# Seven block products for the second channel layer too, on one core

## The chip, the cores and the metric

One core of one Trainium2 chip runs the kernel in a single launch. The metric is the device time of one execution in microseconds (us). The engines are named as the profile names them: PE (TensorE, matrix products into PSUM), DVE (VectorE), ACT (ScalarE), POOL (GpSimd), SP (SyncE, which only issues transfers here). Each takes its instructions in the order in which they stand in its own queue, and semaphores join the queues.

## The reference

The input is `x`, 8 sequences of 3008 tokens with 256 features. A Fourier mixing comes first (`rfft` over the tokens, a complex 256 x 256 product, a soft threshold, `irfft`), then a layer over the tokens, then one over the channels:

```python
xt = x.transpose(0, 2, 1)
h = np.maximum(xt @ w_tok1, 0.0) @ w_tok2
u = x + h.transpose(0, 2, 1)
h2 = np.maximum(u @ w_ch1, 0.0) @ w_ch2      # 256 -> 1536 -> 256
return (u + h2).astype(np.float32)
```

The change is in the last two lines: for each token the channel layer takes `u` (256 features) to 1536 hidden values, rectifies them, takes them back to 256 and adds `u`.

## The kernel before

All products are of float32 quality, from two parts: a tensor is held as `hi` (rounded to the shorter format that the fast matmul takes) and `lo` (the rest), and a product is three matmuls, hi x hi, hi x lo and lo x hi (`mm3`, lines 195 to 198). "Product" below always means these three.

**Stages.** The first half, some 1200 us, computes the Fourier mixing and the token layer of the sequences (units 0 to 4: two of one sequence, three of two), and does the channel layer of the first units beside it, in chunks of at most 512 tokens (`channel`). The rest of the tokens are done in 17 **wide chunks** of up to 1024 (`CW7`) in `channel7`; this is the second half of the time. What the wide chunks need of earlier stages (`g`, `b_d`, `wt2_d`) is in DRAM or SBUF by then. In each wide chunk `make_u` forms `u` for the next one from groups of up to 470 tokens (12 matmuls of that width in each half of a group, and up to ten short ones), ACT copies it to `uf`, `sum_u` makes four sums of its blocks on DVE, and `split_u7` splits the seven operands into hi and lo (`ub`; ACT makes hi, DVE lo).

**First layer by seven products.** The 2 x 2 blocks of the first weight matrix (two feature halves by two hidden blocks of 128) and of `u` (two feature halves by two halves of the chunk's tokens, up to 512 each) are multiplied by seven products in place of eight, in a scheme of Strassen's kind: sums of weight blocks (`ws`, made by `weigh` in the last narrow chunk) times sums of blocks of `u`. `first7(n, p)` does this for one pair `p` of hidden blocks; there are six pairs. The products go to four banks of PSUM (`sx`, `sw`, `sq`, `sz`; `sx` is written three times). ACT and DVE bring the partial sums to SBUF (`sn`), and `rectify` makes hi and lo of the rectified hidden block (`hh` on ACT, `hlo` on DVE).

**Second layer by plain products.** `second7` multiplies each of the 12 hidden blocks, for each token half, with the two output halves of its weights (`w2h`, `w2l`, resident in SBUF) and sums over all 12 in PSUM (`po`, four banks). So a chunk has 42 products in the first layer and 48 in the second. `finish7` adds `uf` and stores the chunk.

**Order.** The code is a loop over pairs: `first7` of a pair, `second7` of the pair before, `make_u` of the next chunk in between. A scheduler puts each engine's instructions in order from that; PE's too, within the dependencies.

## Time and profile before

| | |
|---|---|
| three runs | 2392.57, 2396.88 and 2397.1 us; median 2396.88 |
| the profiled execution | span 2395.2 us from the first to the last instruction; its own time is known by this span alone, 1.7 us under the median of the runs |
| instructions | 32192, of them 12542 matmuls |
| granted PE clock | 0.998 in the mean |
| PE waits for another engine, wide stage | none listed between 1205 us and the end |
| DMA | 173 GB/s up to 1200.6 us, 57 GB/s from there to 2379.7 us |

How to read it: "busy" of an engine counts its instructions' time from start to end; a matmul's end is modelled, and one starts before the last has ended, so a sum of durations says less of PE than the distance between starts. Where PE never waits, the other engines' idle time costs nothing.

### The profile page before, as it was taken

What the parts mean: (1) busy time and instruction counts of PE and PEld (TensorE: products, weight loads), DVE (VectorE), ACT (ScalarE), POOL (GpSimd) and SP (SyncE); (2) the same over time, 40 slices, a digit from 0 to 9 for tenths busy, and PEclk for the clock granted to TensorE, in tenths of its full rate; (3) what the DMA queues carried; (4) which work ended last, traced back from release to release, by engine and by line L of the source; (5) the groups of instructions that cost most, each with busy time, mean ns of one, the idle gap of its engine ahead of it and who ended that gap; (6) DMA issues with size and microseconds to landing.
All of it is one profiled execution on the core that took longest, in us unless ns stands there. A gap on an engine that the chain in (4) does not pass through costs nothing.

```text
span 2395.2 us, 32192 instructions
## 1 busy us (share of the span) xinstructions
PE 2361.0 (99%) x12542; PEld 2065.4 (86%) x12542; DVE 1401.9 (59%) x2189; ACT 1129.6 (47%) x2002; POOL 252.5 (11%) x223
## 2 busy tenths in 40 slices
PE   8999999999999999999999999999999999999999
PEld 7878998999888888899888888898888889888887
DVE  7976666655546554655555555555555555555554
ACT  6764445544435443434344444444444444444543
POOL 0000332222213221222000000000000000000000
PEclk9999999999999999999999999999999999999999
DMA  8875477655555554442413112121211112221100
GB/s 210 253 230 155 164 226 220 187 177 165 162 166 159 157 170 159 135 156 97 131 53 90 57 55 62 31 82 60 91 57 38 56 53 82 60 87 61 39 1 35
DMA packets 149767, 277.06 MB, mean 116 GB/s; under 512 B 10934, under 2 KB 94734, under 8 KB 149614
## 3 DMA queue, kind: packets, MB, share of 16 engines
q1 hardware_dynamic: 115225, 208.40, 29.4%
q10 hardware_dynamic: 34388, 66.60, 8.2%
q8 instruction: 99, 1.62, 0.3%
q14 instruction: 55, 0.44, 0.1%
HBM read 177.57 MB, written 97.39 MB: 115 GB/s over the span
## 4 chain that ended last, share of the span: by engine, by line
PE 88%; DVE 4%; DMA 4%; ACT 2%; issue 1%; SPq 1%; POOL 0%; ACTq 0%; DVEq 0%; POOLq 0%
PE po L196 10%; PE po L197 10%; PE po L198 10%; PE pu L860 5%; PE sx L196 3%; PE sx L197 3%; PE sx L198 3%; PE px L482 3%; PE ph L196 3%; PE ph L198 3%; PE ph L197 2%; PE pm L196 2%; PE pm L198 2%; PE pm L197 2%; PE sw L196 2%; PE sw L197 2%
## 5 line engine op out<-in xcount | busy, mean ns | idle before, releaser
L196 PE MATMUL po<-hh,w2h 128*128 128x512 f32 (+5 forms) x1176 | 453.5, 386 | 1.2 <-DVE o L965 0.9
L197 PE MATMUL po<-hlo,w2h 128*128 128x512 f32 (+5 forms) x1176 | 449.9, 383 | 3.3 <-DVE hlo L899 3.3
L198 PE MATMUL po<-hh,w2l 128*128 128x512 f32 (+5 forms) x1176 | 449.6, 382 | 0.0
L1032 ACT ACTIVATE hh<-sn 128x512 fp32r<-128x512 f32 (+2 forms) x408 | 256.2, 628 | 81.7 <-DVE sn L1052 53.3
L1033 DVE SCALAR_TENSOR_TENSOR hlo<-sn,hh 128x512 fp32r<-128x512 f32 (+2 forms) x408 | 275.4, 675 | 9.4 <-ACT hh L1032 0.7
L197 PEld LDWEIGHTS po<-hlo,w2h 128*128 128x128 f32 x1176 | 221.6, 188 | 40.7 <-DVE hlo L899 4.5
L196 PEld LDWEIGHTS po<-hh,w2h 128*128 128x128 f32 x1176 | 221.4, 188 | 38.2 <-ACT xf L484 1.0
L198 PEld LDWEIGHTS po<-hh,w2l 128*128 128x128 f32 x1176 | 221.4, 188 | 37.9
L1041 DVE TENSOR_TENSOR sn<-sq,sn 128x512 f32<-128x512 f32 (+2 forms) x102 | 69.5, 682 | 272.5 <-PE sq L198 255.2
L1037 ACT COPY sn<-sx 128x512 f32<-128x512 f32 (+2 forms) x102 | 59.2, 580 | 323.8 <-PE sx L198 323.8
L899 DVE SCALAR_TENSOR_TENSOR hlo<-ph,hh 128x512 fp32r<-128x512 f32 (+4 forms) x180 | 114.2, 637 | 108.5 <-ACT hh L898 107.1
L149 DVE TENSOR_TENSOR xtl<-xf,xth 128x768 fp32r<-128x768 f32 x84 | 85.2, 1014 | 116.4 <-ACT xth L146 116.1
L898 ACT ACTIVATE hh<-ph 128x512 fp32r<-128x512 f32 (+4 forms) x180 | 100.0, 557 | 112.2 <-PE ph L198 107.3
L196 PE MATMUL pm<-wmh,xth 128*128 128x256 f32 x504 | 145.7, 289 | 3.8 <-ACT xth L146 2.1
L867 ACT COPY uf<-pu 128x470 f32<-128x470 f32 (+16 forms) x152 | 60.5, 425 | 181.2 <-PE pu L860 180.5
L197 PE MATMUL pm<-wml,xth 128*128 128x256 f32 x504 | 142.5, 283 | 0.0
L198 PE MATMUL pm<-wmh,xtl 128*128 128x256 f32 x504 | 142.4, 284 | 0.0
L196 PE MATMUL ph<-uh,w 128*128 128x512 f32 (+4 forms) x360 | 137.1, 382 | 3.9 <-DVE hlo L899 3.2
L860 PEld LDWEIGHTS pu<-g,b 96*128 96x128 f32 x1024 | 130.8, 192 | 3.6 <-DMA b<-b_d 0.3
L197 PE MATMUL ph<-ul,w 128*128 128x512 f32 (+4 forms) x360 | 133.8, 372 | 0.0
L198 PE MATMUL ph<-uh,w 128*128 128x512 f32 (+4 forms) x360 | 133.8, 372 | 0.0
L860 PE MATMUL pu<-g,b 96*128 96x94 f32 x1024 | 129.3, 272 | 0.0
(185 smaller groups left out, 5128.7 us busy)
## 6 DMA issues: line engine op xcount, KB each, us to landing
wt<-wt_d SPq DMA_DIRECT2D x28, 940.0 KB, 5.7
x<-in_x SPq DMA_DIRECT2D x39, 480.0 KB, 4.6
wt<-ws_d SPq DMA_DIRECT2D x36, 512.0 KB, 3.8
a<-a_d SPq DMA_DIRECT2D x36, 512.0 KB, 5.4
b_d<-bt ACTq DMA_DIRECT2D x36, 512.0 KB, 5.1
a_d<-a ACTq DMA_DIRECT2D x36, 480.0 KB, 3.8
wt<-wt_d SPq DMA_DIRECT2D x21, 752.0 KB, 5.0
b<-b_d SPq DMA_DIRECT2D x32, 480.0 KB, 6.4
```

The lines of the kernel that those rows point to most:

```text
L149: lo_eng.tensor_tensor(out=lo, in0=src, in1=hi.bitcast(F32), op=ALU.subtract)
L196: PE.matmul(out, lhsT=wh, rhs=xh, start=start, stop=False, skip_group_check=more)
L197: PE.matmul(out, lhsT=wh, rhs=xl, start=False, stop=False, skip_group_check=more)
L198: PE.matmul(out, lhsT=wl, rhs=xh, start=False, stop=stop, skip_group_check=more)
L482: PE.matmul(pt[:, o:o + 128], lhsT=x, rhs=f2cols(2 * kp + ab), start=True, stop=True)
L860: PE.matmul(pt[:, s * TOKS:(s + 1) * TOKS], lhsT=b2[:, s, cs], rhs=g2[:, 0 if s0 + s == 0 else 1], start=False, stop=s == k - 1)
L867: S.copy(out=ufs[m][:, ct, lo - at:hi - at], in_=pt[:, lo - c0:hi - c0])
L898: S.activation(out=hh, in_=pt, func=AF.Relu)
L899: V.scalar_tensor_tensor(out=hlo, in0=pt, scalar=0.0, in1=hh.bitcast(F32), op0=ALU.max, op1=ALU.subtract)
L1032: S.activation(out=hh, in_=t, func=AF.Relu)
L1033: V.scalar_tensor_tensor(out=hlo, in0=t, scalar=0.0, in1=hh.bitcast(F32), op0=ALU.max, op1=ALU.subtract)
L1041: V.tensor_tensor(out=snap[0], in0=q, in1=snap[0], op=ALU.add)
```

## The change

`second7` now does the second layer by seven products too, over pairs of hidden blocks, token halves and output halves: a chunk has 42 products in either layer. To that end:

- `first7` leaves the four blocks of a pair (`c11`, `c22`, `r12`, `r21`) in float32 in SBUF, not split. It works on groups of three pairs (`TRIO`), and gives way after each product. One of the old snapshots goes, since the order of products is new and `sx` is written four times; three banks in place of four.
- The second layer works group by group, one group behind the first layer. For each of seven operands `r` and each of three pairs `k`, `prepare` makes the operand's sum (DVE) and its hi (ACT) and lo (DVE or POOL), five steps (`LEAD`) ahead, into one of six slots `rh`, `rl`. `product` multiplies it with weights that `weights2` loads from DRAM, three pairs summed in PSUM in one of three banks (`sbanks`). When an operand's three products are done, DVE adds the bank to a quarter of `uf`. In the second group the quarter is then stored.
- A step is one product of the first layer and one of the second, and these, with those of `u`, are pinned: PE runs them as the code writes them (`keep_in_program_order`). `u` has a bank of its own, and its halves are set at numbered steps.
- The sums of both layers' weights are made by `weigh` in the six chunks of unit 1, in 12 small pieces, and go to DRAM (`wsum_d`, `a2_d`); `keep_blocks` copies there those blocks of the second weights that are used as they are. The first layer's sums are read back in the last narrow chunk.

```diff
+TRIO = 3
+LEAD = 5
+AT = (0, 3, 4, 1, 5, 6, 2)
...
+            pt = wc["pu"] if pin else bank("pu")
             for jt in range(2):
-                mm3(pt[:, :n], gh[:, jt, b, cs], gl[:, jt, b, cs], w[:, jt, :n], w[:, 2 + jt, :n], jt == 0, False)
+                if pin:
+                    pinned(pt[:, :n], gh[:, jt, b, cs], gl[:, jt, b, cs], w[:, jt, :n], w[:, 2 + jt, :n], jt == 0)
+                else:
+                    mm3(pt[:, :n], gh[:, jt, b, cs], gl[:, jt, b, cs], w[:, jt, :n], w[:, 2 + jt, :n], jt == 0, False)
+                m = PE.matmul(pt[:, s * TOKS:(s + 1) * TOKS], lhsT=b2[:, s, cs], rhs=g2[:, 0 if s0 + s == 0 else 1], start=False, stop=s == k - 1, skip_group_check=pin)
+                if pin:
+                    tc.keep_in_program_order(m)
...
+            if n in early_sums and f in (4, 8):
+                weigh(*early_sums[n][f // 8])
+            if n in early_sums and f == 11 and early_sums[n][0][0]:
+                keep_blocks(early_sums[n][0][1] // 4)
...
+                if seven and 4 <= f < 10:
+                    DMA.dma_start(out=wc["ws"][:, f - 4].rearrange("p k h f -> p (k h f)").bitcast(F32), in_=wsum_d[:, f - 4])
-                if seven and f in (1, 3, 5):
-                    weigh(f // 2)
...
+    def weigh(kind, p):
...
+        V.tensor_tensor(out=a, in0=both[0].bitcast(F32), in1=both[1].bitcast(F32), op=ALU.add)
+        a11, a12, a21, a22 = (a[:, j, i * 128:(i + 1) * 128] for i in range(2) for j in range(2))
+        s1, s2, s3, s4 = (sf[:, i] for i in range(4))
...
+        V.tensor_tensor(out=s3, in0=a11, in1=a21, op=ALU.subtract)
+        V.tensor_tensor(out=s4, in0=a12, in1=s2, op=ALU.subtract)
+        split(so[:, :, 0], so[:, :, 1], sf, S, V)
+        if kind == 0:
+            DMA.dma_start(out=wsum_d[:, p], in_=so.rearrange("p k h f -> p (k h f)").bitcast(F32))
...
+            DMA.dma_start(out=a2_d[g].rearrange("r p k w -> k p r w")[k, :, 3:], in_=so.rearrange("p k h f -> p k (h f)").bitcast(F32))
+    def keep_blocks(g):
+        for r, (i, j) in enumerate(((0, 0), (0, 1), (1, 1))):
+            for n, name in enumerate(("w2h", "w2l")):
+                fs = wc[name][:, 2 * TRIO * g:2 * TRIO * (g + 1)].rearrange("p (k j) c -> p k j c", j=2)
+                DMA.dma_start(out=a2_d[g, r][:, :, n * 128:(n + 1) * 128], in_=fs[:, :, j, i * 128:(i + 1) * 128].bitcast(F32))
...
+    def pinned(out, wh, wl, xh, xl, start):
+        for n, (w, x) in enumerate(((wh, xh), (wh, xl), (wl, xh))):
+            m = PE.matmul(out, lhsT=w, rhs=x, start=start and n == 0, stop=n == 2, skip_group_check=True)
+            tc.keep_in_program_order(m)
+    def first7(n, g):
-        x, w, q, z = (bank(k)[:, :h] for k in ("sx", "sw", "sq", "sz"))
...
-            pos[n] = [ps1.tile([128, 2, 512], F32, tag=tag, name="po") for tag in ("po", "gp")]
-        for k in order:
-            hh, hlo = hs[f, k]
-            for ct in range(2):
-                cs = slice(ct * 128, (ct + 1) * 128)
-                mm3(pos[n][k][:, ct, :h], wc["w2h"][:, 2 * p + f, cs], wc["w2l"][:, 2 * p + f, cs], hh, hlo, p + f == 0, 2 * p + f == NF - 1)
...
+        for k in range(TRIO):
+            p = TRIO * g + k
+            c11, c22, r12, r21 = (t[:, k, :h] for t in blocks)
+            x, w, q = (bank(name)[:, :h] for name in ("sx", "sw", "sq"))
...
+            def product(out, a, i, start):
+                pinned(out, *left(p, a), ubs[i][:, 0, :h], ubs[i][:, 1, :h], start)
+            product(x, 4, 0, True)
+            S.copy(out=c11, in_=x)
+            yield
+            product(w, 0, 1, True)
+            S.copy(out=c22, in_=w)
+            yield
+            product(x, 1, 2, False)
+            S.copy(out=r12, in_=x)
+            yield
+            product(q, 5, 3, True)
+            V.tensor_tensor(out=c11, in0=q, in1=c11, op=ALU.add)
+            yield
+            product(x, 2, 4, False)
+            V.tensor_tensor(out=c22, in0=x, in1=c22, op=ALU.add)
+            yield
+            product(w, 3, 5, False)
+            V.tensor_tensor(out=r12, in0=w, in1=r12, op=ALU.add)
+            S.activation(out=r12, in_=r12, func=AF.Relu)
+            yield
+            product(x, 6, 6, False)
+            S.activation(out=r21, in_=x, func=AF.Relu)
+            yield
+    def weights2(g, r):
+        a = wc["seven"].tile([128, TRIO, 2, 128], F32R, name="a2s", bufs=3)
+        DMA.dma_start(out=a.rearrange("p k h f -> p (k h f)").bitcast(F32), in_=a2_d[g, AT[r]].rearrange("p k w -> p (k w)"))
+        return a
...
+    def second7(n, g, blocks, odd):
+        banks = wc["sbanks"]
+        x, w, q = (banks[i][:, :h] for i in ((2, 1, 0) if odd else (0, 1, 2)))
+        outs = (x, w, x, q, x, w, x)
+        homes = ((0, 0), (1, 1), (0, 1), (0, 0), (1, 1), (0, 1), (1, 0))
+        weights, ready = {}, {}
...
+        def prepare(j, slot):
+            r, k = divmod(j, TRIO)
+            hi, lo = (wc[name][:, slot, :h] for name in ("rh", "rl"))
+            a, b, c, d = (t[:, k, :h] for t in blocks)
+            src = (a, a, a, d, c, b, a)[r]
+            if r == 1:
+                V.scalar_tensor_tensor(out=a, in0=a, scalar=0.0, in1=c, op0=ALU.max, op1=ALU.subtract)
+            if r == 2:
+                V.scalar_tensor_tensor(out=a, in0=b, scalar=0.0, in1=a, op0=ALU.max, op1=ALU.add)
+            if r == 4:
+                V.scalar_tensor_tensor(out=c, in0=b, scalar=0.0, in1=c, op0=ALU.max, op1=ALU.subtract)
+            if r == 6:
+                V.tensor_tensor(out=a, in0=d, in1=a, op=ALU.subtract)
+            if r in (0, 5):
+                S.activation(out=hi, in_=src, func=AF.Relu)
+                V.scalar_tensor_tensor(out=lo, in0=src, scalar=0.0, in1=hi.bitcast(F32), op0=ALU.max, op1=ALU.subtract)
+            else:
+                S.copy(out=hi, in_=src)
+                eng = V if k == 0 and 2 <= r <= 4 else G
+                eng.tensor_tensor(out=lo, in0=src, in1=hi.bitcast(F32), op=ALU.subtract)
+            ready[j] = hi, lo
+        def product(j):
+            r, k = divmod(j, TRIO)
+            if k == 0:
+                fetch(r + 2)
+            hi, lo = ready.pop(j)
+            pinned(outs[r], weights[r][:, k, 0], weights[r][:, k, 1], hi, lo, r in (0, 1, 3) and k == 0)
+            if k == TRIO - 1:
+                i, j = homes[r]
+                o = uf[:, i, j * h:(j + 1) * h]
+                V.tensor_tensor(out=o, in0=outs[r], in1=o, op=ALU.add)
+                if g == 1 and r >= 3:
+                    store7(n, i, j)
+        return SimpleNamespace(prepare=prepare, product=product, fetch=fetch)
...
+        ps3 = ctx.enter_context(tc.tile_pool(name="ps3", bufs=1, space=bass.MemoryType.PSUM, reuse_waits="tile"))
+        wc["sbanks"] = [ps3.tile([128, 512], F32, name=f"s{i}") for i in range(3)]
+        wc["pu"] = ps3.tile([128, 512], F32, name="pu")
+        seconds, count = [], [-7 * TRIO]
...
+        def step():
+            j = count[0]
+            count[0] += 1
+            if j >= 0:
+                seconds[j // 21].product(j % 21)
+                if j % 21 in (19, 20) and j // 21 + 1 < len(seconds):
+                    seconds[j // 21 + 1].fetch(j % 21 - 19)
+            j += LEAD
+            if 0 <= j < 21 * len(seconds):
+                seconds[j // 21].prepare(j % 21, j % 6)
...
+                m = make_parts(g)
+                first = 1 + 6 * i if n == ns[0] else 22 - 9 * (len(mine) - 1 - i)
+                makes[first], makes[first + (3 if n == ns[0] else 4)] = (m, i), (m, i)
+            for g in range(2):
+                f = first7(n, g)
+                blocks = next(f)
+                seconds.append(second7(n, g, blocks, len(seconds) % 2))
+                for t in range(7 * TRIO):
+                    at = 7 * TRIO * g + t
+                    next(f)
+                    step()
+                    if at in makes:
+                        m, i = makes[at]
+                        if next(m, None) is not None and i + 1 < len(mine):
+                            load_wt2(mine[i + 1])
+                            load_b2(mine[i + 1])
+                    if at == 33:
+                        load_ahead(n + 2)
+                    if after:
+                        if at == 30:
+                            sum_u(after)
+                        if at in (32, 34):
+                            split_u7(after, at // 2 - 16)
+                        if at >= 37:
+                            split_u7(after, at - 35)
+        for _ in range(7 * TRIO):
+            step()
```

**The order on PE**, in the middle of the wide stage. Before, the seven products of a pair stand together (here the last two, into `sz` and `sx`), and behind them the eight of the second layer (`po`; `hh`, `hlo` are the hidden block's two parts):

```order
L196 MATMUL sz<-ub,w_963 128x512
L197 MATMUL sz<-ub,w_963 128x512
L198 MATMUL sz<-ub,w_963 128x512
L196 MATMUL sx<-ub,ws 128x512
L197 MATMUL sx<-ub,ws 128x512
L198 MATMUL sx<-ub,ws 128x512
L196 MATMUL po<-hh_18455,w2h 128x512
L197 MATMUL po<-hlo_18456,w2h 128x512
L198 MATMUL po<-hh_18455,w2l 128x512
```

Now (s_11429 and s_11431 are banks of the second layer, `a2s` its weights, `pu` the forming of `u`):

```order
L1059 MATMUL sx<-ub,ws 128x512 x3
L1059 MATMUL s_11429<-rh,a2s 128x512
L1059 MATMUL s_11429<-rl,a2s 128x512
L1059 MATMUL s_11429<-rh,a2s 128x512
L1059 MATMUL sw<-ub,ws 128x512 x3
L1059 MATMUL s_11431<-rh,a2s 128x512
L1059 MATMUL s_11431<-rl,a2s 128x512
L1059 MATMUL s_11431<-rh,a2s 128x512
L1059 MATMUL sx<-ub,w_965 128x512 x3
```

The two layers now alternate product by product, and between the end of one product into `sx` and the start of the next stand three others (two of the second layer, one into `sw`).

**The order on DVE**, from one add out of `sq` on, once a pair. Before (`hlo` is the lo of a hidden block, `sn` a partial sum):

```order
L1041 TENSOR_TENSOR sn<-sq,sn 128x512
L1046 TENSOR_TENSOR sn<-sw,sn 128x512
L1033 SCALAR_TENSOR_TENSOR hlo_16944<-sn,hh_16943 128x512
L1051 TENSOR_TENSOR sn<-sx,sn 128x512
L1033 SCALAR_TENSOR_TENSOR hlo_16952<-sn,hh_16951 128x512
L1052 TENSOR_TENSOR sn<-sx,sn 128x512
L1033 SCALAR_TENSOR_TENSOR hlo_16965<-sn,hh_16964 128x512
L1033 SCALAR_TENSOR_TENSOR hlo_16969<-sn,hh_16968 128x512
```

Now, the first 13 of the 16 instructions up to the next such add (c_18451 to r_18454 are the blocks of the group before, c_18744 and on those of the group in work):

```order
L1085 TENSOR_TENSOR c_18744<-sq,c_18744 128x512
L1124 SCALAR_TENSOR_TENSOR c_18451<-c_18452,c_18451 128x512
L1088 TENSOR_TENSOR c_18745<-sx,c_18745 128x512
L1135 TENSOR_TENSOR rl<-r_18454,rh 128x512
L1126 SCALAR_TENSOR_TENSOR r_18453<-c_18452,r_18453 128x512 x3
L1091 TENSOR_TENSOR r_18746<-sw,r_18746 128x512
L1147 TENSOR_TENSOR uf<-s_11430,uf 128x512
L1128 TENSOR_TENSOR c_18451<-r_18454,c_18451 128x512 x2
L1135 TENSOR_TENSOR rl<-r_18453,rh 128x512
L1128 TENSOR_TENSOR c_18451<-r_18454,c_18451 128x512
```

Four adds a pair out of the first layer's banks have become three (L1085, L1088, L1091), and between them now stand the preparation of the second layer's operands, with both inputs in SBUF, and the adds of finished outputs (L1147).

On POOL nothing stood in this stage; now it has 24 instructions a full chunk, all of one kind:

```order
L1135 TENSOR_TENSOR rl<-c_20170,rh 128x512 x3
L1135 TENSOR_TENSOR rl<-c_20456,rh 128x512 x5
L1135 TENSOR_TENSOR rl<-r_20459,rh 128x512 x2
L1135 TENSOR_TENSOR rl<-r_20458,rh 128x512 x2
L1135 TENSOR_TENSOR rl<-c_20456,rh 128x512 x3
```

They make the lo part of those operands that are not left to DVE (`eng` in `prepare`).

More of the change, by code (lines that the diff above doesn't have):

```diff
@@ L138, in tile_kernel @@
     ps = ctx.enter_context(tc.tile_pool(name="ps", bufs=4, space=bass.MemoryType.PSUM))
-    ps1 = ctx.enter_context(tc.tile_pool(name="ps1", bufs=1, space=bass.MemoryType.PSUM))
+    sums = ExitStack()
+    ps1 = sums.enter_context(tc.tile_pool(name="ps1", bufs=1, space=bass.MemoryType.PSUM))
     def bank(name):
@@ L1057, in tile_kernel @@
-    pos = {}
-    def second7(n, p, hs, f, order):
-        h = chunks[n][2] // 2
-        if n not in pos:
-            pos[n] = [ps1.tile([128, 2, 512], F32, tag=tag, name="po") for tag in ("po", "gp")]
-        for k in order:
-            hh, hlo = hs[f, k]
-            for ct in range(2):
-                cs = slice(ct * 128, (ct + 1) * 128)
-                mm3(pos[n][k][:, ct, :h], wc["w2h"][:, 2 * p + f, cs], wc["w2l"][:, 2 * p + f, cs], hh, hlo, p + f == 0, 2 * p + f == NF - 1)
-    def finish7(n, k, step):
+        blocks = [wc["tail"].tile([128, TRIO, CW], F32, tag="blk", name=k, bufs=8) for k in ("c11", "c22", "r12", "r21")]
@@ L1072, in finish7 @@
         uf = us[n][0]
[L1073 to L1080 removed]
+        for b, bi in enumerate(UNITS[u]):
+            lo, hi = max(at + j * h, b * N), min(at + (j + 1) * h, (b + 1) * N)
+            if lo < hi:
+                DMA.dma_start(out=outv[bi][:, i:i + 1, lo - b * N:hi - b * N], in_=uf[:, i:i + 1, lo - at:hi - at])
     def load_ahead(n):
@@ L1087, in load_ahead, with tasks_of @@
             load_b2(needs[n][0])
+    def tasks_of(first):
+        tasks = [(kind, p) for kind in range(2) for p in range(NF // 2)]
+        return {first + i: tasks[2 * i:2 * i + 2] for i in range(len(tasks) // 2)}
+    early_sums = tasks_of(min(n for n, (u, _, _) in enumerate(chunks) if u == 1))
     def channel7(ns):
@@ L1091, in channel7 @@
         wc["tail"] = ctx.enter_context(tc.tile_pool(name="tail", bufs=1, reuse_waits="tile"))
-        behind = None
-        half = NF // 2
+        for name, old in (("rh", "w2h"), ("rl", "w2l")):
+            wc[name] = const.tile([128, 2 * TRIO, CW], F32R, tag=old, name=name)
+        sums.close()
+        ps3 = ctx.enter_context(tc.tile_pool(name="ps3", bufs=1, space=bass.MemoryType.PSUM, reuse_waits="tile"))
[12 more added lines that the diff above has]
+                seconds[j // 21].prepare(j % 21, j % 6)
         for n in ns:
```

118 lines of the change are left out of this document (34 added, 84 removed).

## The prediction

> **What bounds the kernel now.** I read the views in this order: the page, the busy times by stage, the timeline of TensorE (PE) for its pace, the groups by shape for the price of one operation, and last the places where two engines meet. The stage that the change touches begins with the first product into `sx`, at 1200.6 us:
>
> ```profile
> L196 PE MATMUL sx<-ub,w x102: 361/389/469, 1200.6 to 2375.0; 128*128 128x512 f32 x84, 128*128 128x448 f32 x12, 128*128 128x490 f32 x6
> ```
>
> ```profile
> PE 2361.0 (99%) x12542; PEld 2065.4 (86%) x12542; DVE 1401.9 (59%) x2189; ACT 1129.6 (47%) x2002; POOL 252.5 (11%) x223
> ```
>
> ```profile
> core 0: us, PE busy (x) PEld busy (x) DVE busy (x) ACT busy (x) POOL busy (x), PEclk, DMA share, GB/s
> 0.00:1200.60 1200.60, 1170.76 (x6837) 1048.74 (x6838) 735.42 (x1161) 565.76 (x974) 252.52 (x223) 1.00 0.57 173
> 1200.60:2379.70 1179.10, 1179.10 (x5659) 1007.77 (x5658) 660.55 (x1020) 561.80 (x1025) 0.00 (x0) 1.00 0.19 57
> ```
>
> In the second stretch, the 17 wide chunks, PE is busy for all of 1179.1 us. VectorE (DVE) is busy 660.6 us, 56%, ScalarE (ACT) 48%, GpSimd (POOL) not at all; the granted clock is 1.00. So here the time is the number of matmuls times their pace. The 389 ns of a matmul row are not that pace, since matmuls overlap; it is read from starts:
>
> ```profile
> 2379.77 0.39 PE L196 MATMUL po<-hh,w2h 128*128 128x512 f32 x1
> ...
> 2384.53 0.39 PE L196 MATMUL po<-hh,w2h 128*128 128x512 f32 x1
> ```
>
> 21 matmuls lie between these starts: 4.76 / 21 = 0.2267 us each. A product is three of them, 0.68 us.
>
> **What goes.** A chunk of 1024 tokens has 126 matmuls of 512 columns in the first layer, and 144 in the second (12 blocks, 2 halves, 2 outputs, 3 each). The second falls to 7 x 6 x 3 = 126, so 18 go. The 17 chunks are 980, 4 x 1024, 896, 5 x 1024, 896 and 5 x 1024 tokens, 17108 in all; the halves add up to 8554 columns. 18 x 8554 / 512 x 0.2267 = **68.2 us** off PE. This term is firm; the rest asks how much of it comes back as waiting.
>
> **What comes: work on three engines.** By the code, a full chunk has on DVE 18 adds from PSUM in the first layer, 42 operations that prepare operands, 14 adds of finished outputs, 4 sums and 7 splits of the next chunk: 85. On ACT it has 30 + 42 + 7 and some 5 copies of `uf`: 84. On POOL it has 24 subtractions, where none were. Their prices:
>
> ```profile
> 2011.08 0.68 DVE L999 TENSOR_TENSOR t<-uf,t 128x512 f32<-128x512 f32 x1
> 2011.68 0.68 DVE L1000 TENSOR_TENSOR t<-uf 128x512 f32<-128x512 f32 x1
> ```
>
> ```profile
> 1370.34 0.59 ACT L1043 COPY sn<-sx 128x512 f32<-128x512 f32 x1 [0.83 <-PE sx L198]
> 1370.82 0.63 ACT L1032 ACTIVATE hh<-sn 128x512 fp32r<-128x512 f32 x1
> 1371.70 0.59 ACT L1049 COPY sn<-sz 128x512 f32<-128x512 f32 x1 [0.24 <-PE sz L198]
> ```
>
> ```profile
> L149 POOL TENSOR_TENSOR yl<-z,yh x72: 1267/1292/1707, 462.7 to 1145.1; 128x512 fp32r<-128x512 f32 x72
> ```
>
> Behind one another, DVE operations start every 0.60 us, and ACT's 0.48 after a copy (I take 0.54 over the mix). POOL takes 1.29. So DVE has 85 x 0.60 = 51 us a chunk, ACT 84 x 0.54 = 45, POOL 24 x 1.29 = 31. Against them stands PE: 252 x 0.2267 = 57.1, and the forming of `u`, whose half of a group takes 2.3 us from its first matmul to that of the other half:
>
> ```profile
> 1499.98 0.37 PE L196 MATMUL pu<-wt,gh 128*128 128x470 f32 x1
> ...
> 1502.30 0.46 PE L196 MATMUL pu<-wt,gh 128*128 128x470 f32 x1
> ```
>
> With two groups in the chunk (the commoner case) that is 57.1 + 4 x 2.3 = 66.3 us. By sums alone every engine fits beneath PE, DVE at 77%. But the engines work in a fixed order, and now they meet at two places.
>
> **First meeting: a bank.** PE writes `sx` four times a pair and must not write before the last content is read. Between the end of one product into it and the next stand three products in the new order, 2.04 us. Of this go the tail of the last matmul (0.39 - 0.23 = 0.16), the handover to the reader, and the reader:
>
> ```profile
> 2378.86 0.39 PE L198 MATMUL sz<-ub,w 128*128 128x512 f32 x1
> ```
>
> ```profile
> 2379.34 0.59 ACT L1049 COPY sn<-sz 128x512 f32<-128x512 f32 x1 [0.24 <-PE sz L198]
> ```
>
> The matmul ends at 2379.25 and the copy starts at 2379.34: 0.09. With a DVE add of 0.69 and one more handover, 2.04 - 0.16 - 0.18 - 0.69 leaves about **1.0 us by which DVE may be late** before PE stands. PE no longer has loose work to put there: both layers' products and those of `u` are pinned in program order.
>
> **Second meeting: DVE and POOL.** They get in each other's way, and the trace shows when:
>
> ```profile
> 386.31 0.69 DVE L250 TENSOR_TENSOR sd<-x 120x512 f32<-120x512 f32 x1 [1.60 <-DMA x<-in_x]
> 386.35 1.81 POOL L249 TENSOR_TENSOR sd<-x 120x512 f32<-120x512 f32 x1 [7.02 <-DMA x<-in_x]
> 386.92 1.65 DVE L167 SCALAR_TENSOR_TENSOR wide<-wide 128x376 uint32<-128x376 uint32 x1
> ```
>
> ```profile
> 395.83 0.54 DVE L899 SCALAR_TENSOR_TENSOR hlo<-ph,hh 128x376 fp32r<-128x376 f32 x1
> 396.29 1.19 DVE L149 TENSOR_TENSOR wt<-wide,wt 128x376 fp32r<-128x376 f32 x1
> ```
>
> ```profile
> L899 DVE SCALAR_TENSOR_TENSOR hlo<-ph,hh x180: 533/647/693, 159.1 to 1197.6; 128x512 fp32r<-128x512 f32 x72, 128x470 fp32r<-128x470 f32 x48, 128x376 fp32r<-128x376 f32 x36, 128x448 fp32r<-128x448 f32 x12
> ```
>
> ```profile
> L519 DVE TENSOR_TENSOR z<-z x84: 676/693/1780, 238.5 to 1142.8; 128x512 f32<-128x512 f32 x84
> ```
>
> At 386 the first DVE operation keeps POOL back by 0.5 us (1.81 against 1.29), and POOL then keeps the next one back by 1.1 (1.65 against the 0.54 that 128x376 takes at 395.83). At 396.29 one is kept back by 0.65, behind one that ran freely. L899, which reads one operand from PSUM, is never over 693 ns; L519, both operands in SBUF, goes up to 1780. So two-SBUF operations and POOL's exclude each other, and PSUM-fed ones pass. Here 42 + 4 + 7 = 53 of the 85 are of the excluded kind: 53 x 0.60 + 31 = 63 us a chunk that can't overlap. What one POOL operation costs DVE, b, lies between 0 (it falls wholly beside PSUM-fed adds or idle time; the median of L519 is the plain price) and 1.1 (386.92). I take **b = 0.5**: nearer to the row at 396.29, where a PSUM-fed operation comes first, as 32 of 85 do here, and a little below it, because some fall into idle time.
>
> **The sum.** From one add `sq` to the next, the order shows on DVE 16, 14, 12, 20, 12 and 11 operations in a two-group chunk (85). POOL has 4, 5, 3, 4, 5 and 3 in these stretches, by which steps its operands are prepared. PE has 7 x 1.36 = 9.5 us in each, plus 2.3 for each half of `u`: 9.5, 9.5, 11.8, 14.1, 11.8 and 9.5. DVE, at 0.60 and b = 0.5, needs 11.6, 10.9, 8.7, 14.0, 9.7 and 8.1. It is late by 2.1, then by 1.4 more; 1.0 is slack, so PE stands **2.5 us a chunk**, and the other four stretches fit. 16 chunks that follow a full one: **40 us**.
>
> Smaller terms. While the first 21 products have no second layer between them, one product (0.68) separates two uses of `sx`, less than a copy and its handovers: some 0.3 us, three or four times a pair, three pairs, partly covered by `u`: +3. After the last first-layer product, 21 second products (14.3 us, counted in PE's sum) run with 28 DVE operations at 0.6 + b x 12, 23 us, of which five steps are done before: +2. In the first half, 12 weight sums replace 3, and 18 stores of weight blocks stand in SyncE's queue ahead of loads; PE has 30 us idle there already and DVE is at 61%: +2, from 0 to 15. The six reloads of `ws` and the 14 loads of second-layer weights a chunk (393 KB each) are asked for six steps, 8.2 us, ahead:
>
> ```profile
> wt<-ws_d SPq DMA_DIRECT2D x36, 512.0 KB, 3.8
> ```
>
> These 512 KB loads of the first half landed in 3.8 us, at a DMA share of 0.57 against the wide stage's 0.19. I count them at nothing; if each were late by half a microsecond, 14 x 16 x 0.5 = 112 us would come.
>
> Together -68.2 + 40 + 3 + 2 + 2 = -21: 2395.2 - 21 = 2374 of span, and 1.7 more, by which the median of the runs stands over the profiled span: **2376 us**.
>
> **Rivals.** *Little exclusion.* The order puts POOL's work where it meets adds from PSUM; b = 0.1. Then the first stretch is late by 0.5, within the slack, and PE never stands: -68 + 7, **2336**. For it: in the first half, 223 POOL operations leave a mean of 1014 ns on L149's `xtl` (x84) where a free one takes 0.96; so most met nothing:
>
> ```profile
> L149 DVE TENSOR_TENSOR xtl<-xf,xth 128x768 fp32r<-128x768 f32 x84 | 85.2, 1014 | 116.4 <-ACT xth L146 116.1
> ```
>
> ```profile
> 1102.57 0.96 DVE L149 TENSOR_TENSOR xtl<-xf,xth 128x768 fp32r<-128x768 f32 x1 [4.07 <-ACT xth L146]
> ```
>
> Against it: there DVE and POOL had room, here 63 of 66 us are taken.
>
> *DVE, held by POOL, becomes the bound.* With b = 0.8 the six stretches need 12.8, 12.4, 9.6, 15.2, 11.2 and 9.0 us: late 3.3 + 2.9 - 1.0, and 0.1 in the fourth, 5.3 a chunk, 85 us: -68 + 85 + 7 = +24, **2421**. It decides from 61 / 16 = 3.8 us a chunk, that is b = 0.64, little above my value. At b = 1.1 it would be near 2500. The Trainium skill, page "SBUF — State Buffer", section "Who interferes with whom", states that a VectorE instruction with two SBUF inputs contends with a GpSimd one that reads SBUF, and the section "SBUF: two separate sides" that whoever starts first holds the pair for the whole instruction and the other fully blocks. By that rule this rival is the likelier the fuller both engines are; the rows at 386 agree with it, 0.5 and 1.1 us.
>
> *The weights come late*, +112 less what hides it: **2480** at the worst, for which only the thin margin of the drain speaks.
>
> **How the numbers follow.** The forecast with b from 0.35 to 0.6 (2355 to 2392) gets 0.43; little exclusion 0.16; near the point of balance, within 0.2% (4.8 us, about what a measurement of this kernel can tell from no change), 0.08; DVE and POOL as the bound 0.28, late weights 0.05. So faster 0.59, same 0.08, slower 0.33. The range, 2336 to 2440, leaves out the far end of the last two.
>
> **What would show it.** The changed profile should have 306 matmuls fewer; PE idle of 30 to 50 us in the wide stage, before products into `sx` and `sw`, released by DVE or ACT; DVE near 85% busy there, its two-SBUF lines with means of 0.75 to 0.9 us and PSUM-fed ones at 0.69; POOL's subtraction at 1.5 to 2 us. I am wrong if PE's gaps end at POOL or at DMA, if the two-SBUF lines stay at 0.69, or if the first 1200 us have grown by more than a few.

## The result, and the profile after

| | median, us | runs |
|---|---|---|
| before | 2396.99 | 2392.57 to 2400.70 (4) |
| changed | 2488.51 | 2481.83 to 2493.84 (4) |

The ratio is 1.0381, with a 95% interval of 1.0356 to 1.0407: 91.5 us slower. The forecast was 2376 us, its range ended at 2440. The page of the changed kernel (its span was 2492.1 us), first the busy times, then the chain that ended last:

```profile
PE 2364.7 (95%) x12236; PEld 2032.4 (82%) x12236; DVE 1843.5 (74%) x2650; ACT 1336.6 (54%) x2419; POOL 855.0 (34%) x631
...
PE 53%; DVE 30%; ACT 7%; DMA 4%; issue 3%; POOL 2%; SPq 1%; ACTq 0%; POOLq 0%; DVEq 0%
```

The 306 matmuls are gone (12542 to 12236), yet PE now stands for a twentieth of the span, and DVE holds 30% of the chain. By stage, with the granted clock (PEclk) third from the end:

```profile
core 0: us, PE busy (x) PEld busy (x) DVE busy (x) ACT busy (x) POOL busy (x), PEclk, DMA share, GB/s
0.00:1200.60 1200.60, 1165.41 (x6772) 1042.52 (x6773) 749.01 (x1203) 560.63 (x971) 258.01 (x223) 0.99 0.60 184
1212.50:2370.00 1157.50, 1083.00 (x4992) 898.42 (x4991) 984.88 (x1305) 701.22 (x1315) 531.86 (x365) 0.97 0.43 129
```

The wide stage begins at 1212.5 us, 12 later than before. In it PE lacks 74 us of 1157; before it lacked none. DVE is at 85%, as forecast, and not full. Who PE waits for from 1220 us on (sum, times, longest):

```profile
PE sx L1059 <- DVE c L1088: 73.1, 54, 3.4
PE sx L1059 <- ACT c L1076: 5.8, 6, 1.1
PE s L1059 <- POOL rl L1135: 5.6, 7, 1.7
PE pu L1059 <- DMA wt<-wt_d: 3.2, 1, 3.2
```

One wait is nearly all of it: the next product into `sx` waits until DVE has added `sx` to `c22` (L1088). Second-layer weights (`a2s`) are never late. One such wait, engine by engine from the timeline (start, duration), DVE first:

```profile
1343.99 0.68 DVE L1147 TENSOR_TENSOR uf<-s,uf 128x512 f32<-128x512 f32 x1
...
1346.39 1.78 DVE L153 TENSOR_TENSOR ub<-t,ub 128x512 fp32r<-128x512 f32 x1
...
1351.69 3.48 DVE L1124 SCALAR_TENSOR_TENSOR c<-c,c 128x512 f32<-128x512 f32 x2
...
1356.30 0.68 DVE L1085 TENSOR_TENSOR c<-sq,c 128x512 f32<-128x512 f32 x1
1356.90 1.15 DVE L1124 SCALAR_TENSOR_TENSOR c<-c,c 128x512 f32<-128x512 f32 x1
1357.97 0.68 DVE L1088 TENSOR_TENSOR c<-sx,c 128x512 f32<-128x512 f32 x1
```

```profile
1345.92 1.70 POOL L1135 TENSOR_TENSOR rl<-c,rh 128x512 fp32r<-128x512 f32 x1 [4.21 <-DVE c L1088]
1351.35 3.28 POOL L1135 TENSOR_TENSOR rl<-c,rh 128x512 fp32r<-128x512 f32 x2 [3.73 <-ACT rh L1133]
1355.91 1.59 POOL L1135 TENSOR_TENSOR rl<-c,rh 128x512 fp32r<-128x512 f32 x1 [1.28 <-ACT rh L1133]
```

```profile
1355.64 0.39 PE L1059 MATMUL s<-rh,a2s 128*128 128x512 f32 x1
1358.70 0.96 PE L1059 MATMUL sx<-ub,w 128*128 128x512 f32 x3 [2.67 <-DVE c L1088]
...
1359.83 0.63 PE L1059 MATMUL s<-rl,a2s 128*128 128x512 f32 x1
1360.25 0.63 PE L1059 MATMUL s<-rh,a2s 128*128 128x512 f32 x1
1360.68 1.49 PE L1059 MATMUL sx<-ub,w 128*128 128x512 f32 x3
```

DVE runs without a break. Beside POOL's two subtractions at 1351.35, two L1124 take 3.48 us where two take 1.28 otherwise; L153 and the third L1124 grow by 1.1 and 0.5. The add is late by the sum of these, and PE stands 2.7 us. Then comes something the prediction has no term for: from 1359.83 the matmuls start 0.42 us apart instead of 0.227. The same place by windows:

```profile
1340.00:1355.60 15.60, 15.35 (x67) 12.07 (x66) 14.94 (x19) 10.34 (x20) 6.45 (x5) 1.00 0.33 100
1355.60:1358.60 3.00, 0.43 (x2) 0.00 (x1) 3.00 (x6) 1.79 (x4) 2.69 (x2) 1.00 0.47 130
1358.60:1362.00 3.40, 3.30 (x10) 2.60 (x11) 3.40 (x5) 1.85 (x4) 3.40 (x3) 0.65 0.00 1
```

After the wait the clock falls to half, in pieces of 3.41 us or twice that. The wide stage has 83 us at half clock; before it had 3, all at the end of the program.

### The profile page after: what moved, and what is told of

The parts are those of the page before. It is cut to its first block, busy times and chain, and to the rows that moved or that the text cites. A ratio compares the mean times of both kernels' runs of the same rounds, so it can differ in the third digit from the quotient of the medians.

```text
span 2492.1 us, 33718 instructions
## 1 busy us (share of the span) xinstructions
PE 2364.7 (95%) x12236; PEld 2032.4 (82%) x12236; DVE 1843.5 (74%) x2650; ACT 1336.6 (54%) x2419; POOL 855.0 (34%) x631
## 4 chain that ended last, share of the span: by engine, by line
PE 53%; DVE 30%; ACT 7%; DMA 4%; issue 3%; POOL 2%; SPq 1%; ACTq 0%; POOLq 0%; DVEq 0%
PE s L1059 6%; PE sx L1059 4%; DVE c L1124 4%; PE pu L873 3%; DVE rl L1131 3%; DVE c L1128 3%; PE ph L200 2%; PE px L488 2%; DVE ub L153 2%; PE po L201 2%; PE ph L202 2%; PE ph L201 2%; PE po L202 2%; DVE uf L1147 2%; PE po L200 2%
## 5 line engine op out<-in xcount | busy, mean ns | idle before, releaser
L1135 POOL TENSOR_TENSOR rl<-c,rh 128x512 fp32r<-128x512 f32 (+2 forms) x272 | 395.0, 1457 | 612.8 <-ACT rh L1133 523.6
L1059 PE MATMUL s<-rh,a2s 128*128 128x512 f32 (+2 forms) x1428 | 561.5, 396 | 0.1
L1059 PEld LDWEIGHTS s<-rh,a2s 128*128 128x128 f32 x1428 | 276.1, 193 | 56.7 <-ACT rh L1133 0.7
L1059 PE MATMUL s<-rl,a2s 128*128 128x512 f32 (+2 forms) x714 | 283.4, 397 | 5.6 <-POOL rl L1135 5.6
L1133 ACT CAST rh<-c 128x512 fp32r<-128x512 f32 (+2 forms) x306 | 187.2, 613 | 142.2 <-DVE c L1124 50.5
L1059 PE MATMUL sx<-ub,w 128*128 128x512 f32 (+2 forms) x612 | 193.8, 428 | 73.3 <-DVE c L1088 73.1
L1135 POOL TENSOR_TENSOR rl<-r,rh 128x512 fp32r<-128x512 f32 (+2 forms) x136 | 204.8, 1519 | 118.8 <-ACT rh L1133 109.5
L1131 DVE SCALAR_TENSOR_TENSOR rl<-c,rh 128x512 fp32r<-128x512 f32 (+2 forms) x204 | 165.4, 815 | 51.9 <-ACT rh L1130 51.5
L153 POOL TENSOR_TENSOR yl<-z,yh 128x512 fp32r<-128x512 f32 x72 | 96.1, 1335 | 301.9 <-ACT yh L150 301.8
L1147 DVE TENSOR_TENSOR uf<-s,uf 128x512 f32<-128x512 f32 (+2 forms) x238 | 159.5, 670 | 42.0 <-PE s L1059 42.0
L1059 PE MATMUL sx<-ub,ws 128*128 128x512 f32 (+2 forms) x612 | 177.1, 398 | 6.2 <-ACT c L1076 5.8
L1059 PE MATMUL sw<-ub,ws 128*128 128x512 f32 (+2 forms) x612 | 172.3, 390 | 0.0
L153 DVE TENSOR_TENSOR xtl<-xf,xth 128x768 fp32r<-128x768 f32 x84 | 85.6, 1019 | 109.9 <-ACT xth L150 109.8
```

What stands on the lines that cost most here:

```text
L153: lo_eng.tensor_tensor(out=lo, in0=src, in1=hi.bitcast(F32), op=ALU.subtract)
L1059: m = PE.matmul(out, lhsT=w, rhs=x, start=start and n == 0, stop=n == 2, skip_group_check=True)
L1131: V.scalar_tensor_tensor(out=lo, in0=src, scalar=0.0, in1=hi.bitcast(F32), op0=ALU.max, op1=ALU.subtract)
L1133: S.copy(out=hi, in_=src)
L1135: eng.tensor_tensor(out=lo, in0=src, in1=hi.bitcast(F32), op=ALU.subtract)
L1147: V.tensor_tensor(out=o, in0=outs[r], in1=o, op=ALU.add)
```

## The experiments

Theory T: POOL's subtractions, which read SBUF, lengthen DVE's two-SBUF instructions; so DVE is late at L1088, PE waits, and the clock drops. Rivals: R1, DVE has too many instructions whatever POOL does; R2, the order of DVE's queue is at fault; W, DVE stands still until POOL releases a block. "Waits" below are summed distances between the starts of neighbouring matmuls over 0.5 us, less the pace of 0.227, from 1220 us on (changed kernel: 100 us).

### What of POOL's work costs

POOL that only writes:

```diff
-                eng = V if k == 0 and 2 <= r <= 4 else G
-                eng.tensor_tensor(out=lo, in0=src, in1=hi.bitcast(F32), op=ALU.subtract)
+                if k == 0 and 2 <= r <= 4:
+                    V.tensor_tensor(out=lo, in0=src, in1=hi.bitcast(F32), op=ALU.subtract)
+                else:
+                    G.memset(lo.bitcast(F32), 0.0)
```

> Of the 24 subtractions per chunk on POOL each becomes a POOL memset of the same tile: POOL keeps its 408 instructions in the wide stage and their tiles and releases, but reads nothing. (The low parts of these operands are zero, so the low-order product of them is left out; PE, ACT and DVE keep every instruction.) Theory T (a POOL instruction that reads and writes beside a two-SBUF instruction of DVE lengthens it by about 0.5 us; DVE's queue then comes late at the add into c22, PE waits 2 to 3 us, and the half clock follows the wait): DVE's 216 us of excess go mostly, with them the waits of sx on c (about 100 us) and the half clock behind them (41 us), so 2335 to 2390 us. Rival R1 (DVE simply has too many instructions per chunk, whatever POOL does): within 2470 to 2500 us. Rival R2 (the wait comes of the order of DVE's queue, where instructions that wait for POOL stand ahead of the add): in between, since POOL's memset is shorter than its subtraction too, 2380 to 2440 us.

Measured **2347.8 us**, ratio to before 0.9786 (0.9771 to 0.9801; the ratios below are to before, too). The waits are 1.8 us. The row of L1124 among the groups (count, sum, mean ns, idle before it), first of the changed kernel, then of this one:

```profile
L1124 DVE SCALAR_TENSOR_TENSOR c<-c,c 128x512 f32<-128x512 f32 (+2 forms) x90 | 107.2, 1206 | 23.7 <-POOL rl L1135 23.6
```

```profile
L1124 DVE SCALAR_TENSOR_TENSOR c<-c,c 128x512 f32<-128x512 f32 (+2 forms) x102 | 67.3, 676 | 1.6 <-ACT rh L1133 0.8
```

With the same instructions on PE, DVE and ACT, 141 us are gone against the changed kernel: R1 falls. But two things went at once, the lengthening and DVE's idle time behind POOL (23.6 us). The next runs part them. The first try was flawed:

```diff
+                    G.memset(lo.bitcast(F32), 0.0)
+                    G.tensor_tensor(out=junk, in0=junk, in1=junk, op=ALU.subtract)
```

> The run in which POOL only writes, and behind each memset one POOL subtraction of 512 columns on a scratch tile of its own (in place, both operands read), which nobody waits for. (The low parts made on POOL are zero, their product is left out.) POOL reads and writes as much as in the change, but nothing on DVE waits for what it reads. Theory T (POOL's reading beside DVE's two-SBUF instructions is what costs): DVE's excess comes back, 0.4 to 0.55 us for each of the 408, and the time is 2430 to 2500 us. Rival W (DVE's queue stands still because it waits for POOL to release a block or a low part): 2340 to 2365 us, as the run with writes alone.

2625.2 us, and it settles nothing: from the second chunk on POOL took up to 14 scratch instructions in a row ahead of a memset, and PE waited for that (`PE s <- POOL rl`, 194 us). Again, with the reads in the one instruction whose place is fixed by its output:

```diff
+                    one, two = (wc["junk"][:, i, :h] for i in range(2))
+                    G.tensor_tensor(out=lo, in0=one, in1=two, op=ALU.subtract)
```

> The run with the scratch subtractions again, without its flaw (there POOL ran the scratch instructions ahead of the memsets and PE waited 194 us for late low parts). Each of POOL's subtractions keeps its output tile, size and place but reads two scratch tiles instead of the block and the high part: one POOL instruction as before, as long as before, and no DVE instruction ever waits for POOL to have read a block. (The low parts made on POOL are zero, their product is left out.) Theory T (POOL reading beside DVE is what costs): 0.4 to 0.55 us of DVE excess for each of the 408, the waits of sx on c are there, 2440 to 2490 us. Rival W (DVE standing still for POOL's release of a block): 2345 to 2370 us.

```diff
+                    few = [t[:, :32] for t in (lo, src, hi.bitcast(F32))]
+                    for again in range(2):
+                        G.tensor_tensor(out=few[0], in0=few[1], in1=few[2], op=ALU.subtract)
+                        if not again:
+                            G.memset(lo.bitcast(F32), 0.0)
+                            G.memset(lo.bitcast(F32), 0.0)
```

> The other half of the pair: each subtraction on POOL becomes a subtraction of 32 columns, two memsets of the whole low part and the subtraction of 32 columns again, about 1.4 us together, with the waits of the change (on the high part, and of DVE on POOL) but little reading. (The low parts made on POOL are zero beyond 32 columns; their product is left out.) Theory T: DVE's excess stays under 0.15 us for each of the 408, 2345 to 2380 us. Rival W: 2440 to 2490 us.

Reading scratch: **2481.5 us** (1.0346, 1.0325 to 1.0368). Waiting without reading: **2396.9 us** (1.0007, 0.9993 to 1.0020). L1124 in the first, and in the second, and PE's waits of the second:

```profile
L1124 DVE SCALAR_TENSOR_TENSOR c<-c,c 128x512 f32<-128x512 f32 (+2 forms) x90 | 86.1, 979 | 0.4 <-ACT rh L1133 0.4
```

```profile
L1124 DVE SCALAR_TENSOR_TENSOR c<-c,c 128x512 f32<-128x512 f32 (+2 forms) x102 | 70.9, 695 | 32.1 <-POOL rl L1140 30.7
```

```profile
PE s L1059 <- POOL rl L1140: 23.7, 15, 3.1
PE sx L1059 <- DVE c L1088: 6.4, 13, 0.6
```

Reads of tiles that no one else touches bring the loss back, within 7 us of the whole, with no idle time of DVE behind POOL. (L1124 is shorter there than in the changed kernel, but all of DVE's two-SBUF instructions together are some 250 us over their plain time, about 0.6 us for each POOL instruction, more than in the changed kernel.) Idle time behind POOL (30.7 us, more than in the changed kernel) without the reads leaves 6.4 us of the wait for L1088. The second run's other 24 us are of its own making: POOL needs 1.78 us for the four instructions (2 x 0.37 and 2 x 0.52) instead of 1.48, so its low parts come late. The time lies between T's range and W's, 17 us above T's, less than these waits. T stands, and W falls for the wait at L1088.

### Order and number of DVE's instructions

```diff
-                eng = V if k == 0 and 2 <= r <= 4 else G
+                eng = V
```

> All subtractions of the low parts go to DVE, POOL is idle in the wide stage: 24 more DVE instructions per chunk, 109 instead of 85. Theory T: without POOL each costs 0.6 to 0.69 us, so 65 to 75 us of DVE per chunk against about 70 us of PE; faster than the change by 20 to 70 us, 2420 to 2470 us, with PE's waits on DVE spread over the chunk and shorter. Rival R1 (too many DVE instructions): 24 x 0.68 us x 17 chunks = 277 us more DVE, of which most lands on the end: 2550 to 2760 us. Rival R2 (order of DVE's queue): the waits at the add into c22 stay as they are, 2470 to 2520 us.

**2397.6 us**, 1.0001 (0.9991 to 1.0012): 91 us faster than the change with 24 DVE instructions a chunk more. T's range, 2420 to 2470 us, had the direction but too small a gain; R1's and R2's lie above it. The waits are 44 us, L1124 takes 675 ns, and DVE is busy for 954.5 of the 1000 us from 1300 on.

Then DVE's wide stage was pinned in program order, every instruction as the add shown here, and the low part made (`lower`) one step behind the high part; first with POOL, then without:

```diff
+    P = tc.keep_in_program_order
-            V.tensor_tensor(out=c22, in0=x, in1=c22, op=ALU.add)
+            P(V.tensor_tensor(out=c22, in0=x, in1=c22, op=ALU.add))
...
+        def lower(j):
+            r, k = divmod(j, TRIO)
+            hi, lo, src = ready[j]
```

> DVE's wide-stage instructions are kept in the order of the program, and the preparation of an operand is split over two steps (the sum and the high part one step ahead of the low part), so that no instruction that waits for ACT or POOL stands ahead of an urgent add. POOL does what it does in the change. Theory R2 (order): the 2 to 3 us waits of sx at the third and tenth pair steps go, PE's gaps fall from 100 us to 30 to 60 us and the half clock from 41 us to under 15 us: 2400 to 2440 us. Theory T taken alone (exclusion, whatever the order): DVE is as long per stretch as before, and the time stays within 20 us of the change, 2470 to 2500 us.

> The order of the run before, and all low parts on DVE with POOL idle. If both exclusion and order count, this is the fastest of the two: DVE about 109 instructions x 0.62 us = 68 us per chunk against 66 us of PE at full clock, so DVE and PE are about level, 2380 to 2430 us. If only DVE's count matters (R1), as slow as the run with all on DVE, 2550 us or more. If only the order matters, as the run with the order kept, plus what the 24 instructions add.

**2522.5 us** (1.0515, 1.0497 to 1.0532) and **2637.3 us** (1.0995, 1.0968 to 1.1022): both expectations missed. What DVE stood idle for, in the second:

```profile
DVE rl L1152 <- ACT rh L1142: 230.3, 253, 4.2
DVE uf L1163 <- PE s L1069: 20.1, 26, 1.6
```

In an order fixed by hand a low part stands at the head of DVE's queue and waits for ACT, with the urgent add (here L1098) behind it: PE waits for it 179.5 us. R2 fell in the form I gave it: this order is worse than the scheduler's. Whether a better one exists these two runs do not show.

### Load, or one urgent add?

ACT copies `sx` out, and DVE adds later, so that PE never waits for that add:

```diff
-            V.tensor_tensor(out=c22, in0=x, in1=c22, op=ALU.add)
+            S.copy(out=r21, in_=x)
+            V.tensor_tensor(out=c22, in0=r21, in1=c22, op=ALU.add)
```

> The change, with the add into c22 taken out of the way of PE: ACT copies the bank sx into r21 (which is free until the pair's last product), and DVE adds r21 to c22 from SBUF when it comes to it; the next product in sx waits for the copy of 0.58 us alone. POOL, the low parts and all sums stay as in the change; ACT gets 6 instructions more per chunk, and six of DVE's PSUM-fed adds become two-SBUF adds, which POOL can lengthen. Theory S (the loss is one urgent add with one step of slack behind a queue that keeps up on the whole): the waits of sx on c, 73 us, and most of the half clock behind them go: 2390 to 2430 us. Theory L (DVE, with POOL's lengthening, does not keep up over a chunk): the wait turns up at another instruction of DVE's, and the time stays at 2465 to 2500 us.

> The same on the run with all subtractions on DVE. There sx waits 23 us for c, DVE is 95% busy with 65.5 us of instructions per chunk against 66 of PE. Theory S: the 23 us of waits and the half clock behind them go, 2355 to 2380 us, faster than the kernel before. Theory L: DVE at 95% is the bound, 2385 to 2402 us.

With POOL **2509.7 us** (1.0459, 1.0435 to 1.0484), without **2379.7 us** (0.9922, 0.9897 to 0.9947). PE's largest waits, with POOL and then without:

```profile
PE sx L1059 <- ACT c L1076: 79.9, 45, 2.9
```

```profile
PE s L1059 <- DVE rl L1136: 9.8, 27, 0.7
PE s L1059 <- ACT rh L1134: 4.1, 7, 1.1
PE pu L1059 <- DMA wt<-wt_d: 3.8, 3, 3.1
```

With POOL the wait only moves: ACT stands behind another late add (its relu waits 166 us for L1092), and its copy L1076 is late in turn. The wait moves as theory L has it: DVE doesn't keep up, urgent add or not. But the time lies 10 us above L's range too; six of DVE's adds a chunk now have both inputs in SBUF, and what that costs was not parted. Without POOL the wait for the add is gone, 18 us are won, and this is the one version that computes the reference and is faster than both kernels, by 0.8% and 4.4%. L's figure for it (2385 and up) fell; S's range (up to 2380) held by a hair.

### Fewer, longer DVE instructions

```diff
+            if k == TRIO - 1:
+                his, los = (t[:, first:first + TRIO, :h] for t in (rh, rl))
+                V.tensor_tensor(out=los, in0=blocks[src][:, :, :h], in1=his.bitcast(F32), op=ALU.subtract)
```

> A version meant as an improvement: all of the second layer's operand work on DVE, POOL idle, and three pairs at a time: one instruction of 3 x 512 columns for the low parts of three pairs and one for their block sums. Of the 109 DVE instructions per chunk 44 go. Two instructions of the profiles (1.23 us for 1024 columns, 0.68 for 512) give 0.13 us less a pair of neighbours, and DVE's instructions of 512 follow each other at 0.60 us, so 0.05 to 0.07 us saved for each of the 44: 2.2 to 3 us of DVE per chunk, 62.5 to 63.3 in place of 65.5 against 66 of PE. If DVE's work is what bounds the run with all on DVE (69 us per chunk): 2350 to 2375 us. Rival (an instruction of 1.7 us that cannot be passed stands ahead of the urgent adds, so PE waits longer than now): 2410 to 2460 us.

> As the version by threes, with the block sums left one pair at a time: 28 of the 109 DVE instructions go. If DVE's work bounds: 1.4 to 1.9 us of the 3 us per chunk come back, 2360 to 2380 us. If the long instructions ahead of the adds decide: nearer to the version by threes than to the run with all on DVE, 2400 to 2440 us.

> The version by threes with the early weight sums at the sixth and tenth feature step of a narrow chunk in place of the fourth and eighth. In the run with the early weights alone PE waits 4.7 us at 978 us: the second of two sums takes the buffer of the chunk's output, whose store is still under way (DVE 4.6 us on the store), and ACT, which stands behind that sum, makes PE's operand late. Two steps later the store has landed: 5 to 8 us faster than the version by threes. If another buffer is late instead, the same within 3 us.

**2488.4**, **2434.0** and **2488.2 us** (1.0379, 1.0152 and 1.0382): the hope fell in all, and the first lies above its rival's range as well. PE's waits in the first:

```profile
PE s L1059 <- DVE rl L1143: 74.7, 36, 3.2
...
PE sx L1059 <- DVE c L1088: 3.6, 9, 0.5
```

Not the add is late, as the rival had it, but the low parts themselves. The second run's time lies in its rival's range, but there, too, PE waits for low parts (51.8 us) and not for the add (0.6). By the code the three come only with the third high part, two steps after the first, which leaves the first three steps of the five; that this margin is what lacks was not tried by itself. The third run moved the weight sums and won nothing (0.3 us): PE then waits 6.4 us for a hidden block (`po <- hlo`) in the first 1200 us instead of 3.9.

### The clock

```diff
+            if k == 0:
+                for m in range(5):
+                    tc.keep_in_program_order(PE.matmul(q, lhsT=left(p, 6)[0], rhs=ubs[6][:, 0, :h], start=True, stop=True, skip_group_check=True))
             product(x, 6, 6, False)
```

> The change, with five spare matmuls of 512 columns (1.13 us together) ahead of the product that waits in each group's first pair (34 groups; they write a bank that is free then, and their result is not used). In the change 21 of the 24 waits of 1.8 us or more fall at these two places of a chunk. Theory C (the half clock of 3.4 us behind each such wait costs time of its own, and comes of the idle time before it): the idle part falls to 1.0 to 1.9 us, most of the 83 us at half clock go, and of their 41 us of cost 30 to 36 come back, against up to 15 us of spare matmuls at the 13 places without a long wait: 2452 to 2475 us, granted clock 0.99. Rival (the half clock is only how the records show the wait, or comes whatever fills it): 2488 to 2505 us, clock 0.98.

**2497.5 us** (1.0424, 1.0406 to 1.0441). The half clock did go, from 83 to 27 us, and the clock rose to 0.992; the time did not follow. Whom PE waits for now:

```profile
PE sx L1059 <- DVE c L1088: 28.8, 43, 1.4
PE sq L1096 <- DVE c L1085: 11.5, 12, 1.1
PE s L1059 <- DVE uf L1150: 11.0, 9, 1.3
PE sw L1059 <- DVE r L1091: 11.0, 5, 2.5
```

The waits are shorter and at more places, most of them for DVE: 85 us in sum, besides 38.5 us of spare matmuls (170 x 0.2267, where the expectation counted up to 15 as lost). So the idle time does bring the half clock. What undoing it gave back the time alone cannot tell, since the spare matmuls cost PE time of their own; the stretches of a chunk, in the section on why the prediction was wrong, put it at 10 us at most.

### The early part alone

> The kernel before, with only the early part of the change: the block sums of the second channel weights, their stores, the three stores of the plain blocks (keep_blocks) and the reload of ws in the last narrow chunk; the wide stage is that of before. The prediction priced this part at 2 us; the profile of the change shows its wide stage beginning 12 us later than before (1212.5 against 1200.6). If the early part is the cause: 2405 to 2412 us. If it comes of what the changed wide stage needs first (its pools and first loads): 2396 to 2401 us.

(The edit puts `weigh`, `keep_blocks` and the reloads of `ws` as in the change into the kernel before, and nothing else.) **2405.7 us**, 1.0044 (1.0030 to 1.0058): 9 us. By the start of the same matmul PE is 2.5 us late at 150 us, 6.6 at 250 and still 5.5 at 950, then 12.3 at 1000. In the change's trace the 18 stores of plain blocks are issued between 158 and 195 us; that they cost the 4 us there was not tried by itself. The place near 975, from the timeline:

```profile
966.46 0.39 SPq L976 DMA_DIRECT2D out<-o  x1
...
975.25 0.69 DVE L994 TENSOR_TENSOR sums<-w2h,w2l 128x512 f32<-128x512 f32 x1 [4.57 <-DMA out<-o]
...
977.08 0.62 ACT L147 CAST so<-sums 128x512 fp32r<-128x512 f32 x1 [4.95 <-DVE sums L1004]
977.60 0.83 ACT L147 CAST xth<-xf 128x768 fp32r<-128x768 f32 x1
...
978.48 0.58 PE L197 MATMUL pm<-wmh,xth 128*128 128x256 f32 x1 [4.71 <-ACT xth L147]
```

The sums take the buffer of the chunk's output, whose store is under way; ACT's next instruction waits for the sums, and behind it stands the cast that PE needs.

### All runs together

Time against the waits and the half clock of the wide stage, all in us; the last column is the first run's time plus the differences in waits and in half of the time at half clock:

| run | us | waits | half clock | sum |
|---|---|---|---|---|
| POOL only writes | 2347.8 | 2 | 6 | |
| all on DVE, add not urgent | 2379.7 | 29 | 9 | 2377 |
| POOL slow, little read | 2396.9 | 43 | 31 | 2401 |
| all on DVE | 2397.6 | 44 | 14 | 2394 |
| lows by three | 2434.0 | 76 | 29 | 2433 |
| POOL reads scratch | 2481.5 | 101 | 60 | 2474 |
| by three, sums later | 2488.2 | 104 | 82 | 2488 |
| by three | 2488.4 | 103 | 68 | 2480 |
| **the change** | 2488.5 | 100 | 83 | 2485 |
| change, gaps filled | 2497.5 | 85 | 27 | 2480, with 38.5 of spare matmuls |
| change, add not urgent | 2509.7 | 118 | 83 | 2503 |
| change, DVE in order | 2522.5 | 129 | 101 | 2522 |
| POOL reads scratch, flawed | 2625.2 | 233 | 205 | 2678 |
| no POOL, DVE in order | 2637.3 | 217 | 191 | 2656 |

The sum counts a wait within a piece of half clock twice. Of the waits in the last two rows 90 and 31 us lie within such pieces, in the others at most 16.

## Why the prediction was wrong

- **The 68.2 us of matmuls** were right. Without POOL's reads the changed kernel takes 2347.8; less the 9.3 of the early part that is 2338.5, against 2334 from the prediction's -68, +3 and +2. Its rival "little exclusion" is this run, but for the early part.
- **b, POOL's price to DVE**, was right on the mean: DVE's two-SBUF instructions exceed their plain duration (0.68 us at 512 columns) by 216 us in the wide stage, over 408 POOL instructions 0.53 us (0.5 forecast); POOL's means are 1.46 and 1.52 us, PSUM-fed adds stay at 0.67.
- **The stall, +40, is the step that failed.** The prediction set DVE's work in a stretch between two adds of `sq`, with b = 0.5 for each POOL instruction, against PE's, less 1.0 us of slack, and let four stretches fit. From 1270 us on PE waits 38.7, 16.9, 0, 26.1, 0 and 11.5 us in the six stretches, 2.4, 1.1, 0, 1.6, 0 and 0.7 us a chunk, where 1.1, 1.4, 0, 0, 0 and 0 stood. The trace shows two faults (stretches in the prediction's order, means of a chunk from the second chunk on).

  First, the tally spread b evenly. In the first two stretches POOL's nine instructions took 3.2 and 3.9 us from DVE, 0.79 us each (at 1351.35 two in a row took 2.2), while the three of the third took 0.5 us together. In these two DVE never stands idle (0.01 us), and 16.1 and 14.6 instructions at 0.60 us with what POOL took fill them: they last 12.8 and 12.5 us, where the run whose POOL only writes has 9.6 and 10.5.

  Second, the tally let DVE use all of its time. In the fourth stretch POOL took 2.5 us, near b = 0.5, but DVE also stood idle for 1.8 us, and the stretch lasts 16.3 us against 13.5. The other three differ from that run by at most 0.2 us, though DVE is idle most there (4.4 us in the third, 2.6 in the fifth): idle time in a stretch with room costs nothing, and it can't be carried over into a full one. The changed kernel's largest waits of DVE in this stage, 166 us in these five:

```profile
DVE rl L1131 <- ACT rh L1130: 51.5, 49, 1.7
DVE uf L1147 <- PE s L1059: 42.0, 33, 3.3
DVE ub L153 <- ACT ub L150: 39.5, 15, 6.3
DVE c L1124 <- POOL rl L1135: 25.3, 28, 1.3
DVE c L1128 <- POOL rl L1135: 7.9, 13, 0.7
```

  With the first chunk the waits are 100 us, 60 more than forecast.
- **A term was missing** in PE's time: 83 us at half clock, 40 us by the count above (half of what is over the 3 of before). Little of it is a cost of its own. 68 of the 83 us lie in the second stretch, which DVE fills, and in the third and fifth, which last 11.9 and 11.7 us against 12.0 and 11.5 in the run whose POOL only writes. With the gaps filled these two are 0.3 us shorter each, some 10 us over 16 chunks.
- **The first half, +2**, measured 9 alone by the medians, and 12 in the profiles of that run and of the change. The stores were named; the shared buffer was not seen.
- Drain, first 21 steps and weights: no loss to speak of; PE's longest wait for a transfer was 3.2 us, once. The rival of late weights fell.
- The rival "DVE, held by POOL, becomes the bound" named the mechanism, with 85 us of stall at b = 0.8. Its turning point, b = 0.64, stood for all of POOL's instructions alike; the loss came at a mean of 0.53, because it was 0.79 in the two stretches that decide. The Trainium skill, page "SBUF — State Buffer", section "Who interferes with whom", says that a VectorE instruction with two SBUF inputs contends with a GpSimd one that reads SBUF, not with one that only writes it. Both halves agree here: 0.53 us each for subtractions, 0.01 us for memsets (4.4 us over 405).

Sum: -68 + 100 + 40 + 12 makes +84 of the 97 us between the two spans. The other 13 us, waits under half a microsecond and the end of the program among them, I have not parted.

## What to carry to other kernels

Price what a helping engine takes from the engine it helps: here a POOL subtraction saved DVE 0.60 us, took 0.53 back on the mean, and 0.79 in the stretches that had no room, so that DVE alone did the same work 91 us faster. Where two engines alternate in fixed order, take the price in the stretch that decides and not the mean, and allow for idle time; then ask what stands right ahead of the one instruction that the other engine waits for. Where that instruction frees a bank, letting the engine with room copy the bank out won 18 us with POOL idle; beside POOL's subtractions it lost 21.
